# One of the four sums of each Strassen set is made in the PSUM bank, with an order chosen anew

## The chip, the core and the metric

The kernel runs on one core of one Trainium2 chip. A core has TensorE (PE in the profile, with its weight loads as PEld), VectorE (DVE), ScalarE (ACT), GpSimd (POOL) and SyncE (SP), which each run their own list of instructions in order and wait for one another through semaphores. TensorE writes its products into PSUM banks; VectorE and ScalarE read those banks and write SBUF, and may write a bank too. Transfers between HBM and SBUF are issued here by SP's queue. The metric is the device time of one execution in microseconds (us), the lower the better; a figure for a kernel is the median of its runs.

## The reference, cut to what matters

Attention over 4 batches, 8 heads, 768 positions and a head size of 64, in which a query sees 8 global keys and a local band of 96; then a gated layer without a nonlinear function on the 3072 tokens of 512 features that come out.

```python
scores = scale * np.matmul(q, k.transpose(0, 1, 3, 2)) + bias      # bias falls with distance
scores = np.where(is_global | is_local, scores, -1e9)
a = softmax(scores)                                                # over the keys
attn = np.matmul(a, v)
x = attn.transpose(0, 2, 1, 3).reshape(3072, 512)
out = ((x @ w_a) * (x @ w_b)) @ w_out                              # w_a, w_b 512x1536, w_out 1536x512
```

## The kernel before, in words

The 3072 tokens are cut into six blocks u of 512, and the weights into six pieces fp. A table of 18 passes takes a piece and some blocks at a time. Matmuls run on numbers that are cut into a high and a low part (`xf`, `w`, `hh`, `hl`), so that a float32 product is made of three matmuls: high by high, low by high, high by low. The cut is a CAST (`copy`, L660, to ScalarE at L663 or to VectorE at L665) and a subtraction on VectorE (`tt`, L670, whose instruction is at L673).

The first two passes multiply plainly (`project_plain`, matmul L1458). All later ones use `project` (L1532), which makes the two projections of a piece and a block by seven products in Strassen's manner instead of eight; one such set is named u_fp in the rows, as 5_4, and there are 30 of them. Each product is 12 matmuls of 128x256 (`product` L1430, matmul L1436) into one of two PSUM banks, `al` and `ga`. What comes out of a bank goes to SBUF tiles `s` (three for each set, numbered 0, 1 and 2 in the rows: s1, su and s5 in the code) by `take`, a copy that ScalarE or VectorE does, and by `add`, which adds the bank onto such a tile (VectorE, L1547). The gated product `h` is then made half by half on VectorE, from the two halves of an `s` tile (`times`, L673) or, for one half, from the bank and a copy `sa` of the bank's other half (L1588).

`h` is multiplied by the last weights in `back` (L1614, matmul L1628, tile `acc`), or in the late passes 10 to 17 in Strassen's manner too (`strong_back`, matmul L1688, tiles `m_acc`, `m_psS`, `m_psA`; `quad_back`, L1808, at the very end).

The attention is made in granules, a token block and a pair of heads each, named u_p, as 1_3: scores on TensorE (L1064, `ps`), mask and maximum on VectorE (L1032), exponent on ScalarE (L1048), division by the sum (L1168 on ScalarE in 128x168 pieces, or L1170 on VectorE in one 128x672), a transpose on VectorE (L1198, `tt`), a trip through memory by DMA (`mir`, read back as `px` and `py`), and the values on TensorE (L528, `pa`). Granules of the later blocks lie between the products of the earlier ones.

All these steps are put in one list by a table written in the program, `ORDER` (L127): its numbers say in which order the planned steps are emitted, and each engine works its own steps in that order. A second table, `ON_SCALAR` (L338), names the steps that may go to either ScalarE or VectorE and are to go to ScalarE. No step moves at run time: an engine whose next instruction has to wait stands still.

The core of a set in `project`:

```python
self.product(due, al, w["A11"], x["B11"], True)
take(due + 1 * st, s1, al)
self.product(due + 1 * st, ga, w["A12"], x["B21"], True)
add(due + 2 * st, s1, ga)
```

## Time and profile before

| what | value |
|---|---|
| median of 3 runs | 680.6 us (679.3 to 683.14) |
| the profiled execution: its own time | 684.21 us |
| its span, first to last instruction | 682.4 us |
| granted TensorE clock, mean | 0.994 of full speed |
| busy PE, PEld | 663.9 us (97%), 615.3 us (90%) |
| busy DVE | 631.9 us (93%) |
| busy ACT | 406.6 us (60%) |
| share of PE in the chain that ended last | 79% |

The profile is of one execution, which took 684.21 us by the same clock as the three runs; its span leaves out 1.8 us ahead of the first and behind the last instruction. A busy share is a mean over stages, so the stages are read apart. Records of neighbouring matmuls overlap: twelve matmuls of 128x256 show as 1.59 us although the next twelve begin 1.42 us after them.

### The profile page before, as it was taken

The numbers are of one execution on the slowest core, as the hardware profiler recorded it, in microseconds if no ns is written. First come the engines' busy times: TensorE is split into PE (matmuls) and PEld (weight loads), VectorE is DVE, ScalarE is ACT, GpSimd is POOL, SyncE is SP. The second block draws the span as 40 slices with busy tenths as digits, with TensorE's granted clock in tenths as the row PEclk, the third lists the DMA queues.
The fourth block names the chain that finished last, engine by engine and source line by source line (L and its number), as shares of the span: only waits on it lengthen the run. The fifth ranks groups of instructions, "written<-read, shape, count | busy, mean of one in ns | idle before, by whom it ended". The sixth has DMA issues, their size and how long they took to land.

```text
span 682.4 us, 17619 instructions
## 1 busy us (share of the span) xinstructions
PE 663.9 (97%) x6735; PEld 615.3 (90%) x6735; DVE 631.9 (93%) x1642; ACT 406.6 (60%) x1105; POOL 11.1 (2%) x32
## 2 busy tenths in 40 slices
PE   6899899999999999999999999999999999999996
PEld 5689797779898998999999998999999999999996
DVE  8999898899999999989988978899999999999976
ACT  8998784688894766637666467256455445442310
POOL 1000000000000000000000000000000000000000
PEclk9899998999999999999999999999999999999999
DMA  8879999989999899999998799754545652413252
GB/s 337 296 265 278 314 281 318 325 253 351 332 330 307 297 311 276 311 277 320 263 292 285 232 277 258 221 190 167 152 127 155 211 191 93 126 62 125 67 166 83
DMA packets 78991, 162.48 MB, mean 238 GB/s; under 512 B 7794, under 2 KB 36594, under 8 KB 74546
## 3 DMA queue, kind: packets, MB, share of 16 engines
q1 hardware_dynamic: 78610, 161.05, 74.1%
q8 instruction: 55, 0.90, 0.6%
q14 instruction: 38, 0.31, 0.1%
q10 hardware_dynamic: 288, 0.22, 0.1%
HBM read 108.81 MB, written 52.43 MB: 236 GB/s over the span
## 4 chain that ended last, share of the span: by engine, by line
PE 79%; DVE 6%; issue 5%; DMA 5%; ACT 2%; SPq 1%; POOL 0%; DVEq 0%; ACTq 0%; POOLq 0%
PE al L1436 24%; PE ga L1436 18%; PE acc L1628 14%; PE m_acc L1688 6%; PE m_psS L1688 3%; PE ps L1064 2%; DMA dw_O<-wm 2%; PE ps_al L528 2%; PE m_psA L1688 1%; ACT t L1048 1%; DMA py<-mir 1%; PE ps_ga L528 1%; DMA wr<-wts 1%; PE acc L1808 1%; DVE tt L1198 1%
## 5 line engine op out<-in xcount | busy, mean ns | idle before, releaser
L1628 PE MATMUL acc<-w_O,hh 128*128 128x512 f32 x320 | 114.0, 401 | 0.0
L1436 PE MATMUL al<-xf_T,w_S 128*128 128x256 f32 x720 | 95.7, 282 | 0.0
L1436 PEld LDWEIGHTS al<-xf_T,w_S 128*128 128x128 f32 x720 | 90.3, 188 | 1.3 <-ACT s L663 0.4
L1048 ACT ACTIVATE t<-t,sm 128x168 f32<-128x168 f32 x192 | 81.9, 430 | 13.9 <-DVE sm L1032 13.7
L1628 PEld LDWEIGHTS acc<-w_O,hh 128*128 128x128 f32 x320 | 60.2, 188 | 12.9 <-DVE w_O L673 0.3
L1628 PE MATMUL acc<-w_O,hl 128*128 128x512 f32 x160 | 63.0, 394 | 0.0
L663 ACT COPY s<-al 128x512 f32<-128x512 f32 x55 | 32.1, 584 | 36.7 <-PE al L1436 36.4
L1436 PE MATMUL ga<-xf_T,w_S 128*128 128x256 f32 x360 | 48.2, 283 | 0.2
L1032 DVE CUSTOM_DVE_ANT_0 t<-ps,mask 128x168 f32<-128x168 f32 x160 | 47.8, 326 | 0.6 <-PE ps L1064 0.4
L1436 PE MATMUL al<-xf_T,w_A 128*128 128x256 f32 x360 | 48.1, 283 | 0.1
L1436 PE MATMUL al<-xf_B,w_A 128*128 128x256 f32 x360 | 48.1, 283 | 0.0
L1436 PE MATMUL ga<-xf_B,w_S 128*128 128x256 f32 x360 | 47.9, 282 | 0.0
L1436 PE MATMUL ga<-xf_B,w_A 128*128 128x256 f32 x360 | 47.8, 282 | 0.0
L1436 PEld LDWEIGHTS al<-xf_B,w_A 128*128 128x128 f32 x360 | 45.7, 188 | 1.9 <-DVE sm L1032 0.6
L1168 ACT ACTIVATE t<-t,sm 128x168 f32<-128x168 f32 x124 | 43.2, 425 | 7.0 <-DVE sm L1148 6.8
L1436 PEld LDWEIGHTS al<-xf_T,w_A 128*128 128x128 f32 x360 | 45.5, 188 | 1.3 <-DVE xf_T L673 0.2
L1436 PEld LDWEIGHTS ga<-xf_T,w_S 128*128 128x128 f32 x360 | 45.1, 188 | 1.2 <-DVE s L1547 0.7
L1436 PEld LDWEIGHTS ga<-xf_B,w_S 128*128 128x128 f32 x360 | 45.2, 188 | 0.6
L1547 DVE TENSOR_TENSOR s<-ga,s 128x512 f32<-128x512 f32 x60 | 40.9, 682 | 4.9 <-PE ga L1436 4.8
L1436 PEld LDWEIGHTS ga<-xf_B,w_A 128*128 128x128 f32 x360 | 45.1, 188 | 0.3
L1198 DVE STREAM_TRANSPOSE tt<-t 128x512 f32<-128x512 f32 x80 | 40.3, 550 | 1.4 <-ACT t L1168 1.0
L1064 PEld LDWEIGHTS ps<-qk 64*64 64x64 f32 x960 | 29.4, 141 | 11.5 <-issue 6.2
(383 smaller groups left out, 1535.6 us busy)
## 6 DMA issues: line engine op xcount, KB each, us to landing
wr<-wts SPq DMA_DIRECT2D x21, 1024.0 KB, 7.5
mir<-tt SPq DMA_DIRECT2D x80, 192.0 KB, 4.0
vt<-vd SPq DMA_DIRECT2D x24, 512.0 KB, 6.8
qk<-qk SPq DMA_DIRECT2D x20, 576.0 KB, 7.1
X<-dx SPq DMA_DIRECT2D x11, 1024.0 KB, 6.1
part<-o SPq DMA_DIRECT2D x36, 256.0 KB, 3.7
wl_S<-dw_S SPq DMA_DIRECT2D x36, 256.0 KB, 4.1
px<-mir SPq DMA_DIRECT2D x20, 448.0 KB, 7.1
```

Of the source, the lines that this page charges most:

```text
L528: self.main.nc.tensor.matmul(self.banks[s][64 * h : 64 * h + 64, o : o + 64], self.vt[rows, v0 : v0 + 64], src[rows, 2 * s : 2 * s + 2, 2 ...
L663: self.nc.scalar.copy(out(), src())
L1032: lambda e: nc.vector.tensor_tensor_reduce(t[:, i, h], bank[:, c0 : c0 + KW], self.mask[pair][:, h, kind], -0.125, 3.0e38, ALU.add, ALU.mi ...
L1048: lambda e: nc.scalar.activation(t[:, i, h], t[:, i, h], AF.Exp, bias=sm[:, 0, j : j + 1], scale=-1.0, accum_out=sm[:, 1, j : j + 1],),
L1064: nc.tensor.matmul(bank[64 * s : 64 * s + 64, c0 + c : c0 + c + w], qk[rows, q0 + 64 * s : q0 + 64 * s + 64], qk[rows, k0 + k : k0 + k + w ...
L1168: nc.scalar.mul(flat()[:, j], flat()[:, j], sm[:, 3, j : j + 1])
L1198: nc.vector.transpose(dst[:, :, e0 : e0 + n], src[:, :, c0 : c0 + 32 * n].rearrange("p j (e k) -> p j e k", e=n),)
L1436: self.nc.tensor.matmul(bank[:, ab * HT : ab * HT + HT], w[:, a, (2 * ab + c) * P : (2 * ab + c) * P + P], x[:, b, c], start=first, stop=F ...
L1547: lambda e: nc.vector.tensor_tensor(s[:, :], bank[:, :], s[:, :], op=ALU.add),
L1628: self.nc.tensor.matmul(acc[i][:, :], a[:, rows], w[:, b], start=first and f == 0 and k == 0, stop=False, skip_group_check=True,)
L1688: self.nc.tensor.matmul(bank[:, c * HT : c * HT + HT], fa(k, c * P, c * P + P), fb(l), start=first, stop=False, skip_group_check=True,)
L1808: self.nc.tensor.matmul(acc[i][:, j * HT : j * HT + HT], a[:, rows], ws[j][0](b), start=f == 0 and j == 0 and k == 0, stop=False, skip_gro ...
```

## The change

Only `project` and the two tables are changed. In the code the order of the seven products is another: A11, S1, S2, S4, S3, A22, A12. The sum s1 = A11·B11 + A12·B21 is no longer made by a VectorE addition in SBUF. The first product is still taken out to `s1`, because `al` goes on to hold other sums; later `s1` is copied back into the bank `ga`, after su and s5 are done with it, and the product A12·B21 is added onto it there (`fresh` is False). The half of `h` that came from `s1` is now made from the bank, as the other one was: a copy `sg` of half a bank, and a multiplication of the other half by it (`across`). `sa` and `sg` share one buffer.

```diff
-        self.product(due, al, w["A11"], x["B11"], True)
-        take(due + 1 * st, s1, al)
-        self.product(due + 1 * st, ga, w["A12"], x["B21"], True)
-        add(due + 2 * st, s1, ga)
-        self.product(due + 2 * st, al, w["S2"], x["T2"], False)
-        take(due + 3 * st, su, al)
-        self.product(due + 3 * st, ga, w["S1"], x["T1"], True)
-        take(due + 4 * st, s5, ga)
-        self.product(due + 4 * st, al, w["S3"], x["T3"], False)
-        add(due + 5 * st, s5, al)
-        self.product(due + 5 * st, ga, w["S4"], x["B22"], False)
-        add(due + 6 * st, su, ga)
-        self.product(due + 6 * st, al, w["A22"], x["T4"], False)
-        sa = self.sbuf([P, HT], F32, "sa", "sa" + n, 1)
-        self.copy(due + 7 * st, lambda: sa[:, :], lambda: al[:, :HT], HT, [al], [sa], psum=True)
...
-        times(due + 3 * st, 0, 0, s1)
-        times(due + 6 * st, 1, 1, s5)
-        times(due + 7 * st, 0, 1, su)
-        op(
-            due + 7 * st,
-            lambda e: nc.vector.tensor_mul(h[1][:, :HT], al[:, HT:], sa[:, :]),
...
+        def across(due, f, bank, name):
+            s = self.sbuf([P, HT], F32, "sa", name + n, 1)
+            self.copy(due, lambda: s[:, :], lambda: bank[:, :HT], HT, [bank], [s], psum=True)
+            op(
+                due,
+                lambda e: nc.vector.tensor_mul(h[f][:, :HT], bank[:, HT:], s[:, :]),
+                [bank, s],
+                [(h[f], 0)],
+                dve=dve(HT),
+            )
+
+        self.product(due, al, w["A11"], x["B11"], True)
+        take(due + 1 * st, s1, al)
+        self.product(due + 1 * st, ga, w["S1"], x["T1"], True)
+        take(due + 2 * st, s5, ga)
+        self.product(due + 2 * st, al, w["S2"], x["T2"], False)
+        take(due + 3 * st, su, al)
+        self.product(due + 3 * st, ga, w["S4"], x["B22"], False)
+        add(due + 4 * st, su, ga)
+        self.product(due + 4 * st, al, w["S3"], x["T3"], False)
+        add(due + 5 * st, s5, al)
+        self.copy(due + 5 * st, lambda: ga[:, :], lambda: s1[:, :], T, [s1], [ga])
+        self.product(due + 5 * st, al, w["A22"], x["T4"], False)
+        across(due + 6 * st, 1, al, "sa")
+        self.product(due + 6 * st, ga, w["A12"], x["B21"], False)
+        across(due + 7 * st, 0, ga, "sg")
+        times(due + 5 * st, 0, 1, su)
+        times(due + 6 * st, 1, 1, s5)
```

`ORDER` and `ON_SCALAR` are other numbers throughout; both have no row that could be read by itself. What they do is seen in the lists of the engines. TensorE's lists have the same matmuls and weight loads in both. Lines of the changed kernel are 4 to 7 higher than those of before for the same code (L1436 is L1440, L1547 is L1551, L663 and L665 are L667 and L669).

The first place is set 5_4 on TensorE. A name such as `al5_4_3602` is the bank `al` of set 5_4; the operand behind the comma names the weight part (A11, S2, and so on). Before:

```order
994 L1436 MATMUL ga5_4_3588<-xf1_B21_290313_3476,w4_A12_163548_2638 128x256 x12
995 L1436 MATMUL al5_4_3602<-xf1_B11_290313_3518,w4_A11_163548_2226 128x256 x12
996 L1628 MATMUL acc3_0_3264<-w4_O1_163548_3110,hh4_4_1_3288 128x512
997 L1628 MATMUL acc3_0_3264<-w4_O1_163548_3110,hl4_4_1_3299 128x512
998 L1628 MATMUL acc3_0_3264<-w4_O1_163548_3110,hh4_4_1_3288 128x512
999 L1436 MATMUL al5_4_3602<-xf1_T2_290313_3511,w4_S2_163548_2862 128x256 x12
1000 L1436 MATMUL ga5_4_3588<-xf1_T1_290313_3540,w4_S1_163548_2859 128x256 x12
1001 L1436 MATMUL al5_4_3602<-xf1_T3_290313_3635,w4_S3_163548_2711 128x256 x12
1002 L1436 MATMUL ga5_4_3588<-xf1_B22_290313_3623,w4_S4_163548_3004 128x256 x12
1003 L1436 MATMUL al5_4_3602<-xf1_T4_290313_3688,w4_A22_163548_2504 128x256 x12
```

The same place on TensorE in the changed kernel:

```order
997 L1440 MATMUL al5_4_3593<-xf1_B11_290313_3455,w4_A11_163548_2225 128x256 x12
998 L1440 MATMUL ga5_4_3611<-xf1_T1_290313_3523,w4_S1_163548_2432 128x256 x12
999 L1440 MATMUL al5_4_3593<-xf1_T2_290313_3544,w4_S2_163548_2943 128x256 x12
1000 L1440 MATMUL ga5_4_3611<-xf1_B22_290313_3571,w4_S4_163548_2738 128x256 x12
1001 L1440 MATMUL al5_4_3593<-xf1_T3_290313_3663,w4_S3_163548_2843 128x256 x12
1002 L1440 MATMUL ga5_4_3611<-xf1_B21_290313_3631,w4_A12_163548_3090 128x256 x12
1003 L1440 MATMUL al5_4_3593<-xf1_T4_290313_3674,w4_A22_163548_2371 128x256 x12
```

The product A12 on `ga` has moved from the head of the set to a place behind S4, with one product, S3, between the two.

The second place is VectorE at that set. In the changed kernel (`s5_4_0` is s1, `s5_4_1` is su, `s5_4_2` is s5):

```order
662 L677 TENSOR_TENSOR xT4_1_290313_3666<-X_61,xT2_1_290313_3302 128x512
663 L1551 TENSOR_TENSOR s5_4_1_3669<-ga5_4_3611,s5_4_1_3669 128x512
664 L669 COPY ga5_4_3611<-s5_4_0_3624 128x512
665 L677 TENSOR_TENSOR xf1_T4_290313_3674<-xT4_1_290313_3666,xf1_T4_290313_3674 128x512
666 L1551 TENSOR_TENSOR s5_4_2_3634<-al5_4_3593,s5_4_2_3634 128x512
```

and in the kernel before:

```order
666 L1547 TENSOR_TENSOR s5_4_2_3686<-al5_4_3602,s5_4_2_3686 128x512
667 L673 TENSOR_TENSOR w3_O0_183130_3724<-wl3_O0_183130_3616,w3_O0_183130_3724 128x512
668 L673 TENSOR_TENSOR hl4_3_0_3733<-h4_3_0_3621,hh4_3_0_3706 128x512
669 L745 ISA wm3_5_3460<-wr3_4_3317,wm3_5_3460 128x1024
670 L1547 TENSOR_TENSOR s5_4_1_3670<-ga5_4_3588,s5_4_1_3670 128x512
```

The addition of S4's product onto su is now followed at once by the copy into `ga`, which here stands on VectorE; before, nothing of the set followed it on that bank.

The third place is SP's queue at granule 1_3, where `wr` is a load of raw weights, `qk` and `vt` are loads for later granules, and `part` is a store. Before:

```order
54 L653 DMA qk0_59<-qk 128x1152
55 L653 DMA mir1_3_1654<-tt1_3_1544 32x6x256 x4
56 L689 DMA wr5_2_1673<-wts 128x1024
57 L653 DMA qk1_60<-qk 128x1152
58 L653 DMA px0_272<-mir1_3_1654 112x1024
59 L653 DMA py0_134<-mir1_3_1654 64x512 x2
60 L653 DMA vt2_1_1772<-vd 128x1024
```

In the changed kernel:

```order
55 L657 DMA qk1_60<-qk 128x1152
56 L657 DMA mir1_3_1583<-tt1_3_1542 32x6x256 x4
57 L693 DMA wr5_2_1611<-wts 128x1024
58 L657 DMA vt2_1_1656<-vd 128x1024
59 L657 DMA px0_290<-mir1_3_1583 112x1024
60 L657 DMA py0_140<-mir1_3_1583 64x512 x2
```

The load of `qk1` has moved ahead of the four stores of `mir1_3`, and the load of `vt2_1` from behind the reads of `px` and `py` to a place ahead of them.

## Rows read from the trace of the kernel before

**Rows 1.** The page's busy time (share of the span) and instructions of each engine.

```profile
PE 663.9 (97%) x6735; PEld 615.3 (90%) x6735; DVE 631.9 (93%) x1642; ACT 406.6 (60%) x1105; POOL 11.1 (2%) x32
```

**Rows 2.** By stretch: length, busy PE, PEld, DVE, ACT, POOL, granted clock, DMA share, GB/s.

```profile
100.00:120.00 20.00, 18.36 (x184) 14.60 (x184) 16.78 (x34) 9.39 (x20) 0.00 (x0) 0.91 1.02 324
120.00:220.00 100.00, 100.00 (x1030) 86.80 (x1030) 96.58 (x255) 76.89 (x207) 1.58 (x5) 1.00 0.98 318
220.00:320.00 100.00, 99.90 (x1140) 90.98 (x1139) 93.67 (x242) 61.30 (x176) 2.01 (x5) 1.00 0.94 299
320.00:460.00 140.00, 139.92 (x1477) 129.71 (x1477) 125.05 (x326) 79.69 (x231) 2.40 (x6) 1.00 0.85 253
460.00:560.00 100.00, 99.95 (x839) 99.54 (x838) 97.70 (x224) 52.10 (x113) 0.00 (x0) 1.00 0.54 169
560.00:660.00 100.00, 99.97 (x835) 99.32 (x834) 95.46 (x225) 38.62 (x87) 0.00 (x0) 1.00 0.32 104
```

**Rows 3.** Waits of PE, whole span: who waited for whom: us in total, times, longest.

```profile
PE pa L528 <- DMA py<-mir: 1.6, 1, 1.6
PE ps L1064 <- DMA qk<-qf: 1.6, 1, 1.6
PE ga_1(1,)_1235 L1458 <- DVE h L1504: 1.1, 1, 1.1
```

**Rows 4.** The chain that ended last, 470 to 500 us: start us, us, what.

```profile
475.12 1.43 PE al L1436 x12
476.54 1.58 PE ga L1436 x12
```

**Rows 5.** VectorE by line and shape: count, busy us, mean ns, idle before and releaser.

```profile
L1547 DVE TENSOR_TENSOR s<-ga,s 128x512 f32<-128x512 f32 x60 | 40.9, 682 | 4.9 <-PE ga L1436 4.8
L673 DVE TENSOR_TENSOR h<-s 128x256 f32<-128x256 f32 x90 | 37.3, 418 | 0.7
L1588 DVE TENSOR_TENSOR h<-al,sa 128x256 f32<-128x256 f32 x30 | 12.6, 419 | 4.3 <-ACT sa L663 4.0
L1170 DVE TENSOR_TENSOR t<-t,sm 128x672 f32<-128x672 f32 x9 | 7.7, 856 | 0.5
L665 DVE CAST xf_T<-xT 128x512 fp32r<-128x512 f32 x10 | 4.1, 413 | 0.7 <-PE al L1436 0.7
L665 DVE COPY s<-al 128x512 f32<-128x512 f32 x5 | 3.4, 684 | 0.0
```

**Rows 6.** ScalarE by line and shape, columns as in rows 5.

```profile
L663 ACT COPY s<-ga 128x512 f32<-128x512 f32 x30 | 17.5, 584 | 12.3 <-PE ga L1436 10.8 <-DVE w_O L673 0.8 <-DVE h L673 0.7
L663 ACT CAST xf_T<-xT 128x512 fp32r<-128x512 f32 x38 | 23.5, 620 | 10.5 <-DVE xT L673 10.4
L663 ACT COPY sa<-al 128x256 f32<-128x256 f32 x26 | 9.7, 372 | 47.6 <-PE al L1436 47.5
L1168 ACT ACTIVATE t<-t,sm 128x168 f32<-128x168 f32 x124 | 43.2, 425 | 7.0 <-DVE sm L1148 6.8
```

**Rows 7.** Timeline of PE and VectorE, 499 to 508 us: start us, us, what.

```profile
499.76 1.35 PE L1436 MATMUL ga<-xf_B,w_S 128*128 128x256 f32 x10
504.52 1.59 PE L1436 MATMUL ga<-xf_B,w_A 128*128 128x256 f32 x12
...
502.65 0.68 DVE L1547 TENSOR_TENSOR s<-ga,s 128x512 f32<-128x512 f32 x1
506.26 0.68 DVE L1547 TENSOR_TENSOR s<-ga,s 128x512 f32<-128x512 f32 x1
506.86 0.42 DVE L673 TENSOR_TENSOR xo<-wl_O 128x256 f32<-128x256 f32 x1
```

**Rows 8.** The chain that ended last, 60 to 126 us: start us, us, what.

```profile
98.76 5.13 DMA mir<-tt
...
105.03 7.48 DMA py<-mir
...
114.59 4.45 PE al_0(0, 1)_1793 L1458 x12
...
119.74 3.04 PE al_1(0, 1)_1835 L1458 x12
```

More of the change, by code (lines that the diff above doesn't have):

```diff
@@ L1581, in times @@
             )
-        times(due + 3 * st, 0, 0, s1)
-        times(due + 6 * st, 1, 1, s5)
-        times(due + 7 * st, 0, 1, su)
-        op(
-            due + 7 * st,
-            lambda e: nc.vector.tensor_mul(h[1][:, :HT], al[:, HT:], sa[:, :]),
-            [al, sa],
-            [(h[1], 0)],
-            dve=dve(HT),
-        )
+        def across(due, f, bank, name):
[24 more added lines that the diff above has]
+        times(due + 5 * st, 0, 1, su)
+        times(due + 6 * st, 1, 1, s5)
         parts = []
```

490 rows, old and new, of tables (ON_SCALAR, ORDER) are left out of this document.

## The prediction

> **What bounds the kernel now.** I read the busy time of the engines first, then the same by stretch, then PE's list of waits, then the chain that ended last. The page puts PE at 663.9 us, 97% of the span, and VectorE at 631.9 us, 93% [rows 1]: two engines near full, and the change is about the second. Which of the two sets the end is read from the stretches: from 120 to 660 us PE is busy for 100.00 + 99.90 + 139.92 + 99.95 + 99.97 = 539.7 of 540 us, while VectorE lies between 89% and 98% [rows 2]. A busy record by itself doesn't prove that matmuls follow without loss, since neighbouring records overlap. So I look at their spacing: in the chain a product of 12 matmuls takes 1.43 us, and only now and then 1.58 [rows 4]. No wait of PE is listed from behind 115 us; the ones that are come from the head, 1.6 for the read-back of `py`, 1.6 for the first queries, 1.1 for a reader of a bank [rows 3]. The reader should see here that PE sets the time for four fifths of the span, that it has next to nothing to gain there, and that what can be won or lost lies ahead of 120 us or in waits that are not there yet.
>
> The Trainium skill, Perfetto Trace Analysis, section Identifying the Most-Contended Engine, says that matmul busy time is a poor measure of TensorE's headroom and that the busy share of the weight loads should be taken. By that the share is 90% in place of 97% [rows 1]. I come back to it as a rival.
>
> **The change part by part.** The matmuls are the same in number and shape, so PE's own work costs 0 more and 0 less. All other terms are what PE is made to wait or no longer waits.
>
> VectorE's work. I compared the lists of VectorE in the two orders, kind by kind. Gone: 30 additions `s<-ga,s` at 682 ns, -20.5 us. Exchanged: 30 multiplications `h<-s` at 418 for 30 from the bank at 419, 0 [rows 5]. New or moved over from ScalarE by the table: 4 copies into `ga`; 4 `sg` and 2 more `sa` copies at about 0.42, +2.5; 5 more 512-wide copies out of banks (3 of them `s<-ga`) at 684, +3.4; 12 more 512-wide casts at 413, +5.0; 4 more divisions of 128x672 at 856, +3.4; some small ones, -0.8 [rows 5]. The copy into a bank has no row in the trace of before. From the nearest rows it costs 413 ns (SBUF to SBUF, the CAST) to 684 ns (bank to SBUF, the COPY), for four 1.7 to 2.7 us; I take 684, because one side is a bank. Sum: -20.5 + 2.7 + 2.5 + 3.4 + 5.0 + 3.4 - 0.8 = -4.3 us. Four fifths of the relief is spent at once on work that comes over from ScalarE.
>
> The Trainium skill, VectorE: DVE Perf Modes, section Why PSUM operands drop a tier, says that an operand in PSUM holds a float32 operation at the plain rate. For these four copies that means the higher price, 2.7 us, and without the rule the sum would be -5.3 instead of -4.3.
>
> ScalarE's work. New: 26 copies into `ga`, between 584 (bank to SBUF) and 620 ns (SBUF to SBUF), +15.2 to +16.1 us, and 26 copies `sg` at 372, +9.7 [rows 6]. Gone to VectorE: 16 division pieces at 425, -6.8; 12 casts at 620, -7.4; 5 copies at 584, -2.9; 2 `sa`, -0.7; others about 0. Sum about +7.5. ScalarE is busy for only 60% of the span [rows 1], so the total costs nothing; where its work is dense is the head, below.
>
> What the bank has to hold. This is the new chain: S4's last matmul on `ga`, then the addition onto su (VectorE), then the copy of s1 into `ga`, and only then the first matmul of A12. What PE has between S4 and A12 is the cover. Counted from the new order, at 1.43 us for a product: one product in 2 sets (4_3 and 5_4, both with the copy on VectorE behind the addition), 2.09 to 2.14 us in 8 sets, 2.8 to 2.9 in 7, and 3.5 to 10 in the other 13. The need, in the best case: in the timeline an addition begins 0.15 us after the records of its product end (506.26 against 504.52 + 1.59) and the next instruction of VectorE 0.60 after it (506.86) [rows 7]; 0.15 + 0.60 + 0.68 + some 0.1 for the signal (my estimate, from that same 0.15) is 1.53 us. Since the records of a product reach 0.16 past the start of the next (1.59 against 1.43), one product covers 1.27. So 0.26 short, twice: +0.5 us. In a bad case the addition comes as late as the one at 502.65, 1.54 us after its product's last record (499.76 + 1.35): the need is 2.9, and against the cover less 0.16 the loss is 1.65 in the 2 sets, 0.95 in the next 8, 0.3 in the next 7, 13.0 us in all. Queued behind a copy that waits in ScalarE's list are the takes of the next product, and PE waits for those in turn. Ends +0.5 and +13.0; I take +0.5, because the lists put the additions of the two tight sets where VectorE has few rows ahead of them, and because additions and takes with one product as cover stand in before as well, without a wait of PE from 120 us on.
>
> What VectorE's relief gives back. From 120 to 660 us PE's records leave 0.3 us idle [rows 2]. Products that take 1.58 instead of 1.43 lose 0.15 each [rows 4]; were that so in 20 places, that would be 3 us. Ends 0 and -3; I take -1.
>
> The head. PE lost 1.6 us in front of the values of granule 1_3, and behind it the clock fell: the granted clock is 0.91 of full in the stretch 100 to 120 us, so for a part of it at the lower of its two levels (1.2 instead of 2.4 GHz), and twelve plain matmuls took 4.45 us where the next twelve took 3.04, so 1.4 more [rows 2, 3, 8]. What PE waited for there is a trip through memory, 5.13 us out and 7.48 us back [rows 8], at a DMA share of 1.02 [rows 2]. In SP's list the 1024 KB of raw weights still stand between the way out and the way back, now with the 512 KB of `vt2_1` in place of the 576 KB of `qk1`: 64 KB less at 324 GB/s is 0.2 us. The scores and the values of 1_3 keep their places among PE's work within a microsecond. Ahead of the last division of 1_3 ScalarE has three more casts of `hh` (3 x 0.62 = 1.9 us, rows of the same width in [rows 6]) and half a microsecond of small rows more. I take 0; the ends are -5.0 (1.6 + 1.4, the 1.1 of [rows 3] and its like) and +2.4.
>
> The tail: behind the last product both orders have the same work on PE; 0.
>
> Sum: 684.2 + 0.5 - 1.0 + 0 = 683.7 us for the profiled execution's own time. That execution stands 0.5% above the median of the runs, so as a ratio: 680.6 x 683.7 / 684.2 = 680.1 us. About 0.5%, 3.4 us, is what a measurement of this kernel can tell from no change.
>
> **The rivals.** First, slower: the bank chain. The addition and the copy stand in line on `ga`, and PE waits for A12. It decides from a mean of 0.11 us in each of 30 sets (3.4 us); with half of these 17 sets as in the bad case it is +6.5, and with 1.0 given back 686.1 us. For it speaks that VectorE stays at 96% or so and additions do come 1.5 us late; against it, that the two tightest covers miss by 0.26 only.
>
> Second, slower: the head. ScalarE's 2.4 us more lie on the way to the division of 1_3, the trip through memory starts later and PE waits longer at the lower clock: without any relief 680.6 + 2.4 + 1.4 = 684.4. Against it: ScalarE is idle for half of the stretch from 100 us [rows 2], if a little late for this.
>
> Third, faster: the head loses its waits. If the trip through memory lands 1.6 us earlier, the wait and the slow matmuls go, and with the reader's wait it is -4 to -5, some 676 us. It needs the transfers ahead to be shorter by more than the 0.2 us that I find.
>
> Fourth, faster: PE has headroom from 120 us on, which shows in its weight loads: 86.80 of 100, 90.98 of 100 and 129.71 of 140 us [rows 2]. Then VectorE's 4.3 us could all come back: 676.3. By the Trainium skill, Perfetto Trace Analysis, as named above, that would be so. Against it: from 460 us on the share is 99%, with VectorE as full, and ahead of that the matmuls are of mixed widths, so that a load per matmul leaves more of the time without one.
>
> Fifth, the change doesn't do what it says: VectorE's relief goes to moved work and nothing of it reaches PE: 680.6 + 0.5 = 681.1, no difference.
>
> **How the numbers follow.** My forecast 0.56, the fifth 0.06: together 0.62 within 0.5%. The third 0.14 and the fourth 0.06: faster 0.20. The first 0.12 and the second 0.06: slower 0.18. The range for 8 in 10 reaches into both sides: down to 676.0, at the edge of the third and fourth, and up to 685.5, which takes in the second and half of the first. The forecast's own range is 678 to 683.
>
> **What would show it.** In the changed profile VectorE's busy time should be near 628 us, ScalarE's near 414, PE's unchanged to 1 us; `s<-ga,s` should stand at x30. A copy into `ga` on ScalarE should take 0.58 to 0.62 us. In PE's waits a product on `ga` that waits for a copy may appear with 0.2 to 0.3 us, twice; a total above 3 us there would make the first rival right and me wrong. From 120 us to the last product PE's stretches should be as full as before. If 100 to 120 us shows a granted clock of 1.00 and no wait of `pa`, the third rival holds.

## The result, and the profile after

The changed kernel takes 684.44 us (median of 17 runs, 682.67 to 686.93) against 681.32 for the kernel before (17 runs, 678.26 to 684.25) on the same chip. The ratio is 1.0052 [1.0034, 1.0070], so the change costs 3.1 us by the medians and 3.5 by the ratio, between 2.3 and 4.8 by the interval. The forecast was no change (680.1 us, its own range 678 to 683). The profiled execution of the changed kernel took 685.95 us, 1.5 above its median; that of before stood 2.9 above its own [rows 1 to 8 are of that one], so the two profiles lie only 1.7 us apart and stretches have to be compared over several profiles. The clock is not what sets the kernels apart: the mean granted clock of the 17 executions of the changed kernel is 0.996, and so is that of the 120 executions of the kernel before that were taken along with the experiments. In e15, e16 and e18 below some executions were disturbed; their ratios leave these out, their medians and spreads do not.

The busy time on the page after, which answers to [rows 1]:

```profile
PE 664.3 (97%) x6735; PEld 615.1 (90%) x6735; DVE 628.7 (92%) x1640; ACT 415.1 (61%) x1125; POOL 11.8 (2%) x32
```

VectorE has 3.2 us less to do and ScalarE 8.5 more, PE 0.4 more. By stretch, with the columns of [rows 2] and four stretches of the head added:

```profile
0.00:20.00 20.00, 14.61 (x217) 12.29 (x217) 15.62 (x79) 16.48 (x53) 2.40 (x10) 1.00 0.86 316
20.00:40.00 20.00, 16.00 (x222) 12.63 (x213) 19.59 (x66) 19.64 (x68) 1.44 (x3) 1.00 0.83 302
40.00:60.00 20.00, 18.95 (x234) 17.30 (x233) 19.87 (x69) 19.58 (x61) 0.49 (x1) 1.00 0.89 299
60.00:80.00 20.00, 18.32 (x201) 16.16 (x200) 16.43 (x43) 14.88 (x44) 0.31 (x1) 0.91 0.95 311
100.00:120.00 20.00, 19.44 (x200) 15.77 (x200) 18.62 (x39) 7.57 (x16) 0.00 (x0) 1.00 0.98 319
120.00:220.00 100.00, 99.59 (x1028) 86.27 (x1027) 96.16 (x256) 78.15 (x211) 2.21 (x5) 1.00 0.97 315
220.00:320.00 100.00, 99.22 (x1133) 90.19 (x1133) 92.05 (x237) 63.85 (x179) 1.93 (x5) 1.00 0.92 298
460.00:560.00 100.00, 99.69 (x835) 99.25 (x834) 95.84 (x219) 55.47 (x122) 0.00 (x0) 1.00 0.55 171
560.00:660.00 100.00, 99.85 (x836) 99.30 (x835) 94.41 (x224) 44.35 (x102) 0.00 (x0) 1.00 0.34 109
```

Two things are to be seen. Behind 120 us PE is a little less full in every row shown than in [rows 2], by 0.41, 0.68, 0.26 and 0.12 us. (Not all of that is the change's: e12 below, which has the order of before there, is 0.80 us idle from 220 to 320.) And between 40 and 80 us, which the prediction never looked at, PE stands idle for 2.7 us, while VectorE and ScalarE are full from 20 to 60. The rows of before for these two stretches are

```profile
40.00:60.00 20.00, 19.84 (x240) 18.32 (x241) 19.63 (x65) 19.36 (x58) 0.58 (x1) 1.00 0.75 248
60.00:80.00 20.00, 18.09 (x211) 16.03 (x210) 17.32 (x53) 14.74 (x46) 0.58 (x1) 1.00 0.93 292
```

so that one profile is idle there for 2.1 us too. The other four profiles with this head (e1, e4, e5 and e12) are idle for 0.2 us at most.

PE's waits from 120 us to the end, where before had none:

```profile
PE al L1440 <- DVE s L1551: 0.4, 1, 0.4
PE al L1440 <- DVE sm L1036: 0.4, 1, 0.4
PE ga L1440 <- DVE ga L669: 0.4, 2, 0.2
PE al L1440 <- ACT ga L667: 0.3, 1, 0.3
PE ga L1440 <- ACT ga L667: 0.2, 1, 0.2
```

The third row is the predicted wait, as predicted. It is read best at set 4_3 in the timeline of PE and VectorE:

```profile
236.59 1.12 PE L1440 MATMUL ga<-xf_B,w_S 128*128 128x256 f32 x8
237.55 1.60 PE L1440 MATMUL al<-xf_T,w_A 128*128 128x256 f32 x12
239.35 1.45 PE L1440 MATMUL ga<-xf_B,w_A 128*128 128x256 f32 x10 [0.20 <-DVE ga L669]
...
237.89 0.68 DVE L1551 TENSOR_TENSOR s<-ga,s 128x512 f32<-128x512 f32 x1
238.60 0.69 DVE L669 COPY ga<-s 128x512 f32<-128x512 f32 x1
```

S4's records end at 237.71; the addition begins 0.18 later, the copy 0.71 after it and lasts 0.69, and 0.06 later A12 begins: 1.64 us of chain, where the prediction had put 1.53. Without it A12 would have begun at 237.55 + 1.43 = 238.98; it lost 0.37. The same working gives 0.32 at 5_4, 0.31 at 15_0, 0.26 at 9_2 and 0.13 to 0.06 at three more sets, 1.5 us in seven sets. In the five sets with more cover VectorE has other work first: at 15_0 the addition begins 0.86 us after S4's records end, and at 9_2 a division of 0.85 us stands between the addition and the copy. The first and the fourth row are not the copy's doing. The first is A22 of 6_3, which loses 0.58 because VectorE's addition onto s5 comes late, behind a step that waits 0.8 us for a load of `X`; the fourth is an A22 near 530 us. In e3 below, where no copy goes into the bank, both start just as late, and no A12 loses anything.

PE's waits between 40 and 82 us; the profile of before has none of these there, but the 1.1 us for a reader of a bank [rows 3], 0.8 us in front of a `pa` with no releaser seen, and 0.2 for a ScalarE copy:

```profile
PE acc L1635 <- DVE hl L677: 1.3, 1, 1.3
PE al_1(1,)_890 L1462 <- ACT s_0(1,)_877 L667: 0.9, 1, 0.9
PE pa L532 <- DMA py<-mir: 0.3, 1, 0.3
```

Because single profiles differ, I worked out from the starts of the matmuls how late PE runs: for each matmul the distance to the next one, less the median distance of such pairs over all the profiles of this study. A sum of 30 us is no waiting time, as plain pairs of other kinds are in it too; only differences between kernels count. In us, by stretch of the trace:

| profile | 0–20 | 20–40 | 40–60 | 60–80 | 80–100 | 100–120 | to 120 | behind 120 |
|---|---|---|---|---|---|---|---|---|
| before | 8.4 | 10.2 | 3.5 | 4.4 | 2.3 | 6.1 | 34.9 | 29.2 |
| five profiles with the head of before, mean | 8.5 | 9.8 | 3.3 | 2.7 | 3.4 | 3.5 | 31.3 | |
| after | 9.1 | 9.6 | 4.5 | 5.8 | 2.0 | 3.8 | 34.9 | 31.3 |
| six profiles with the changed head, mean | 9.3 | 9.1 | 4.5 | 5.5 | 2.3 | 3.1 | 33.8 | |
| e3, no copy into the bank | 9.7 | 8.7 | 4.5 | 7.4 | 2.4 | 3.4 | 36.2 | 29.8 |
| e4, before without an addition | 8.7 | 9.2 | 3.2 | 2.7 | 3.4 | 3.0 | 30.2 | 26.9 |
| e12, before with one swap | 8.6 | 10.2 | 3.4 | 2.1 | 3.4 | 2.5 | 30.1 | 30.2 |

(The five are before, e1, e4, e5 and e12, from 29.2 to 34.9 up to 120 us; the six are after, e2, e3, e6, e7 and e8, from 31.4 to 36.2.) The first of the two means is 2.5 us lower, though single profiles of the two groups overlap. In 40–60 no profile of the one group reaches the other: 3.2 to 3.5 against 4.4 to 4.6.

### The profile page after: what moved, and what is told of

The parts are those of the page before. It is cut to its first block, busy times and chain, and to the rows that moved or that the text cites. A ratio compares the mean times of both kernels' runs of the same rounds, so it can differ in the third digit from the quotient of the medians.

```text
span 684.2 us, 17624 instructions
## 1 busy us (share of the span) xinstructions
PE 664.3 (97%) x6735; PEld 615.1 (90%) x6735; DVE 628.7 (92%) x1640; ACT 415.1 (61%) x1125; POOL 11.8 (2%) x32
## 4 chain that ended last, share of the span: by engine, by line
PE 70%; DVE 14%; DMA 5%; issue 5%; ACT 4%; SPq 1%; POOL 0%; DVEq 0%; ACTq 0%
PE al L1440 18%; PE ga L1440 14%; PE acc L1635 13%; PE m_acc L1695 5%; PE ps L1068 3%; PE m_psS L1695 2%; DMA dw_O<-wm 2%; PE ps_al L532 1%; DMA py<-mir 1%; PE pa L532 1%; DMA X<-dx 1%; DVE s L1551 1%; DVE xf_T L677 1%; DVE h L677 1%; ACT t L1052 1%
## 5 line engine op out<-in xcount | busy, mean ns | idle before, releaser
L1440 PE MATMUL al<-xf_T,w_S 128*128 128x256 f32 x720 | 95.5, 282 | 0.0
L1052 ACT ACTIVATE t<-t,sm 128x168 f32<-128x168 f32 x192 | 81.9, 430 | 16.7 <-DVE sm L1036 16.4
L1440 PEld LDWEIGHTS al<-xf_T,w_S 128*128 128x128 f32 x720 | 90.5, 188 | 1.4 <-ACT s L667 0.4
L1440 PE MATMUL ga<-xf_B,w_A 128*128 128x256 f32 x360 | 48.5, 284 | 0.6 <-DVE ga L669 0.4
L1440 PE MATMUL al<-xf_T,w_A 128*128 128x256 f32 x360 | 48.1, 283 | 0.7 <-DVE s L1551 0.4
L1440 PE MATMUL al<-xf_B,w_A 128*128 128x256 f32 x360 | 48.2, 283 | 0.4 <-DVE sm L1036 0.4
L1440 PE MATMUL ga<-xf_T,w_S 128*128 128x256 f32 x360 | 48.0, 282 | 0.0
L1440 PEld LDWEIGHTS al<-xf_B,w_A 128*128 128x128 f32 x360 | 45.5, 188 | 2.6 <-DVE sm L1036 0.8
L1440 PE MATMUL ga<-xf_B,w_S 128*128 128x256 f32 x360 | 47.8, 282 | 0.0
L1440 PEld LDWEIGHTS ga<-xf_B,w_A 128*128 128x128 f32 x360 | 45.2, 188 | 2.9 <-DVE ga L669 1.3
L667 ACT COPY s<-al 128x512 f32<-128x512 f32 x55 | 32.1, 584 | 25.4 <-PE al L1440 25.0
L1440 PEld LDWEIGHTS al<-xf_T,w_A 128*128 128x128 f32 x360 | 45.3, 188 | 1.7 <-DVE s L1551 0.6
L1440 PEld LDWEIGHTS ga<-xf_T,w_S 128*128 128x128 f32 x360 | 45.2, 188 | 0.5 <-DVE xf_T L677 0.2
L1440 PEld LDWEIGHTS ga<-xf_B,w_S 128*128 128x128 f32 x360 | 44.9, 188 | 0.0
L1172 ACT ACTIVATE t<-t,sm 128x168 f32<-128x168 f32 x108 | 37.6, 424 | 4.0 <-DVE sm L1152 3.9
L1068 PE MATMUL ps<-qk 64*64 64x168 f32 (+2 forms) x960 | 34.0, 277 | 2.8 <-DMA qk<-qf 1.9
```

The costliest lines, as they stand in the source:

```text
L667: self.nc.scalar.copy(out(), src())
L1052: lambda e: nc.scalar.activation(t[:, i, h], t[:, i, h], AF.Exp, bias=sm[:, 0, j : j + 1], scale=-1.0, accum_out=sm[:, 1, j : j + 1],),
L1068: nc.tensor.matmul(bank[64 * s : 64 * s + 64, c0 + c : c0 + c + w], qk[rows, q0 + 64 * s : q0 + 64 * s + 64], qk[rows, k0 + k : k0 + k + w ...
L1172: nc.scalar.mul(flat()[:, j], flat()[:, j], sm[:, 3, j : j + 1])
L1440: self.nc.tensor.matmul(bank[:, ab * HT : ab * HT + HT], w[:, a, (2 * ab + c) * P : (2 * ab + c) * P + P], x[:, b, c], start=first, stop=F ...
```

## The experiments

**One head with the other's body.** e1 is the changed kernel in the order of before up to its first Strassen product, e2 the kernel before with the changed head. The edit in short (in the file the table is a list of numbers):

```diff
-ORDER = order_of_this_kernel
+ORDER = head_of_other + [o for o in order_of_this_kernel if o not in head_of_other]
```

> The changed kernel with the order of before up to the first Strassen product (some 120 us) and its own order behind it. Bank theory (PE waits in front of A12 for the addition and the copy into the bank, some 2 us from 120 us on, the rest of the loss in the head): the loss shrinks to about 2 us, a ratio to before near 1.003, and the waits in front of A12 stay in the trace. Head theory (the new order loses its 3 us ahead of 120 us): a ratio of 1.000. If the head plays no part: 1.005 as in the changed kernel.

> The mirror image: the kernel before with the changed kernel's order up to the first Strassen product. Bank theory: only the head's part, about +1 us, a ratio near 1.0015. Head theory: the whole +3 us, 1.005. If the head plays no part: 1.000.

Measured: e1 688.16 us, 1.0093 [1.0064, 1.0122]; e2 685.86, 1.0069 [1.0035, 1.0103]. Both are slower than both kernels, so neither tells what the head alone costs. PE's waits of e1 from 130 us, at the seam of the two orders:

```profile
PE al L1437 <- DVE sm L1033: 1.8, 1, 1.8
PE ga L1437 <- DVE sm L1033: 1.2, 1, 1.2
PE al L1437 <- ACT s L664: 1.1, 1, 1.1
```

Neither kernel has waits of that size there. Between 120 and 200 us e1 runs 12.2 us late by the working above and e2 9.8, the other whole kernels 6.4 to 7.8. The seam hides the answer.

**The chain in the bank.** e3 copies s1 onto itself, and A12 starts its bank afresh; the two instructions stay, the dependence goes. e7 makes the copy into the bank twice.

```diff
-        self.copy(due + 5 * st, lambda: ga[:, :], lambda: s1[:, :], T, [s1], [ga])
+        self.copy(due + 5 * st, lambda: s1[:, :], lambda: s1[:, :], T, [s1], [s1])
...
-        self.product(due + 6 * st, ga, w["A12"], x["B21"], False)
+        self.product(due + 6 * st, ga, w["A12"], x["B21"], True)
```

```diff
-        self.copy(due + 5 * st, lambda: ga[:, :], lambda: s1[:, :], T, [s1], [ga])
+        def into(e):
+            for _ in range(2):
+                (nc.scalar.copy if e == "act" else nc.vector.tensor_copy)(ga[:, :], s1[:, :])
+
+        op(due + 5 * st, into, [s1], [ga], act=act(T), dve=dve(T, True))
```

> The changed kernel, in which the copy of s1 is written onto s1 itself instead of into the bank ga, and A12 starts afresh (one half of h is then wrong). The work of the engines stays about the same, but A12 waits only for the addition of S4. Bank theory: the waits of PE for a copy into ga vanish and some 2 us come back, a ratio near 1.002. Head theory: 1.005 as before.

> The changed kernel with each copy of s1 into the bank made twice in a row on the same engine. Bank theory: about nine A12 products already wait, so each waits some 0.5 us longer, and others begin to: +4 to +6 us against the changed kernel, a ratio to before near 1.012, with the waits in front of A12 grown in the trace. If the copies lie beside PE's work: ScalarE's 15 us more cost nothing, 1.005.

Measured: e3 683.78 us, 1.0021 [0.9990, 1.0052]; e7 693.55, 1.0167 [1.0124, 1.0210]. In e3 no product waits for a copy into `ga`, and behind 120 us PE runs 1.5 us less late than in after (29.8 against 31.3); the ratios differ by 0.0031, 2.1 us, with intervals that overlap. (e10 below, with the same body as after, runs 30.6 us late behind 120 us, so profiles alone differ by 0.7.) The 1.5 us that seven products lose one by one in after, and in e3 none, are the best figure. In e7 the chain shows in PE's waits, behind 120 us:

```profile
PE ga L1440 <- ACT ga L1595: 4.8, 8, 1.2
PE ga L1440 <- DVE ga L1595: 2.7, 3, 0.9
PE al L1440 <- DVE h L1577: 0.4, 1, 0.4
```

Eleven products on `ga` wait 7.5 us, and the kernel loses 9.1 us to after by the medians, 7.8 by the ratios, more than was expected. So the copy is on the path, for some 1.5 us, and a second one of 0.6 us in each set costs about five times that: the covers of more sets no longer reach.

**What VectorE's relief is worth.** e4 leaves the 30 additions onto s1 out of the kernel before, 20.5 us of VectorE [rows 5, half of the x60]. e8 keeps the changed order but makes s1's sum on VectorE as before, without a copy into the bank.

```diff
-        add(due + 2 * st, s1, ga)
+        op(due + 2 * st, lambda e: None, [ga], [s1], dve=dve(T))
```

```diff
-        self.copy(due + 5 * st, lambda: ga[:, :], lambda: s1[:, :], T, [s1], [ga])
+        op(due + 5 * st, lambda e: None, [s1], [ga], act=act(T), dve=dve(T, True))
...
-        self.product(due + 6 * st, ga, w["A12"], x["B21"], False)
-        across(due + 7 * st, 0, ga, "sg")
+        self.product(due + 6 * st, ga, w["A12"], x["B21"], True)
+        op(
+            due + 7 * st,
+            lambda e: nc.vector.tensor_tensor(s1[:, :], ga[:, :], s1[:, :], op=ALU.add),
...
```

> The kernel before without the 30 additions onto s1 (one half of h lacks a product): VectorE has 20.5 us less to do, order and PE's work as before. If VectorE's relief is worth next to nothing because PE is full (my step on the relief, -1 us): a ratio of 0.998 to 1.000. If PE has headroom that VectorE's lateness eats (the fourth rival): several us, 0.99 or lower.

> The changed order with the arithmetic of before: A12 starts afresh on ga, VectorE adds it onto s1 in SBUF where the copy sg stood, no copy into the bank. VectorE has some 19 us more than in the changed kernel, in places that were not chosen for it. If VectorE's relief is worth 0.07 us for each us, as the run without additions says, then -1.6 for the chain and +1.3 for the work: about the changed kernel's time, 1.004 to 1.005. If the new order leans on the relief: 1.01 or more.

Measured: e4 680.45 us, 0.9982 [0.9957, 1.0007]; e8 695.66, 1.0210 [1.0163, 1.0257]. 20.5 us off VectorE bring 0.0018 x 681.3 = 1.2 us and at most 2.9, and by the interval perhaps nothing: 0.06 us for each, at most 0.14. The other way round it is dear: e8 is some 11 us slower than after, with waits of PE on VectorE's `s` (3.5 us, 4 times) and on a ScalarE take (2.0 us, twice). So the changed order, with the additions where e8 puts them, leans on the lighter VectorE, and the order of before hardly uses it.

**The heads by themselves.** e5 and e6 are the two kernels cut off behind the same 826 steps, which are those that both have in their heads (a few of them are moved up, so that these come first); all later steps are left out.

```diff
-            for o in order:
+            for o in order[:826]:
```

> Only the steps that both orders have ahead of the first Strassen product (826 of them: the first two passes and what goes with them), in the order of before; all later steps are left out, so there is no result. It is to be compared with the next run, which does the same steps in the changed order. If the head plays no part the two medians agree within 0.5 us.

> The same 826 steps in the changed kernel's order, all later steps left out. Bank theory with a part for the head: 1 to 2 us above the run before, since the copies were worth 1.6 of the 3.1 us. Head theory: 3 us above. Head without a part: equal.

Measured: e5 160.35 us (159.64 to 160.92), e6 164.60 (164.37 to 166.36): 4.2 us, with no overlap. In the profiles the last matmul ends at 153.9 and 157.7, and 3.7 and 5.1 us of each span lie behind it; that 1.4 is how the cut-off lists end and not a cost of the whole kernel, so 2.8 of the 4.2 remain. (The last matmuls of these two profiles lie 3.8 us apart; that e5 ran below its median there is a part of it.) None of the 826 steps is a Strassen product, so the sum in the bank has no part in this: what the head loses comes of the order chosen anew. By stretch, of e5 and then of e6:

```profile
0.00:20.00 20.00, 14.39 (x219) 12.28 (x219) 16.60 (x83) 16.90 (x53) 2.37 (x10) 1.00 0.91 333
20.00:40.00 20.00, 16.49 (x213) 13.05 (x214) 19.76 (x66) 19.71 (x66) 0.46 (x2) 1.00 0.85 301
40.00:60.00 20.00, 20.00 (x239) 18.45 (x239) 19.88 (x68) 19.33 (x61) 0.57 (x1) 1.00 0.85 267
60.00:80.00 20.00, 20.00 (x230) 18.16 (x229) 19.55 (x58) 16.41 (x53) 1.20 (x2) 1.00 0.98 324
```

```profile
0.00:20.00 20.00, 14.59 (x193) 12.11 (x193) 15.06 (x78) 15.97 (x50) 1.96 (x9) 1.00 0.83 307
20.00:40.00 20.00, 15.92 (x228) 12.66 (x226) 19.54 (x65) 19.60 (x69) 1.80 (x3) 1.00 0.81 298
40.00:60.00 20.00, 18.95 (x239) 17.11 (x236) 19.88 (x67) 19.51 (x59) 0.49 (x1) 1.00 0.87 297
60.00:80.00 20.00, 18.38 (x213) 16.30 (x213) 17.87 (x54) 15.95 (x49) 0.30 (x1) 1.00 0.95 309
```

The head alone shows what the whole kernel shows between 40 and 80 us: PE idle for 2.7 us, where with the order of before it is full in e5. PE's waits of e6 from 40 us on are the same two as in after:

```profile
PE acc L1632 <- DVE hl L674: 1.6, 1, 1.6
PE al_1(1,)_890 L1459 <- ACT s_0(1,)_877 L664: 0.9, 1, 0.9
```

**The waits in the head, one by one.** In after, the 1.3 us for `hl` come about so (timeline):

```profile
68.05 0.66 ACT L707 ACTIVATE wm<-wr 128x512 f32<-128x512 f32 x1 [2.01 <-DMA dw_O<-wm]
68.75 0.43 DVE L714 TENSOR_SCALAR wm<-wm 128x512 f32<-128x512 f32 x1 [1.63 <-ACT wm L707]
69.09 0.41 DVE L677 TENSOR_TENSOR hl<-h,hh 128x256 fp32r<-128x256 f32 x1
69.56 0.50 PE L1635 MATMUL acc<-w_O,hl 128*128 128x512 f32 x1 [1.30 <-DVE hl L677]
```

The half block `hl` is ready to be made, but in VectorE's list it stands behind a step on weights that waits for ScalarE, which waits for a store. e9 exchanges the two; e12 makes the opposite exchange in the kernel before.

```diff
-L714 TENSOR_SCALAR wm2_0_1083<-wm2_0_1083 128x512
 L677 TENSOR_TENSOR hl0_0_1_1046<-h0_0_1_858,hh0_0_1_931 128x256
+L714 TENSOR_SCALAR wm2_0_1083<-wm2_0_1083 128x512
```

```diff
-L673 TENSOR_TENSOR hl0_0_1_1076<-h0_0_1_886,hh0_0_1_1058 128x256
 L710 TENSOR_SCALAR wm2_1_1133<-wm2_1_1133 128x512
+L673 TENSOR_TENSOR hl0_0_1_1076<-h0_0_1_886,hh0_0_1_1058 128x256
```

> The changed kernel with one step moved in its order: on VectorE the subtraction hl0_0_1 (first half) stands ahead of the weight step wm2_0 instead of behind it. Step theory (PE's wait for hl near 68 us comes from VectorE standing at wm2_0, which waits for ScalarE, which waits for a store): the wait of 1.3 to 2.1 us goes, and the kernel gains about as much, a ratio to before near 1.003. Rival: the wait only moves, as VectorE is late there anyway: 1.005 with the same total of waits between 60 and 80 us.

> The mirror image in the kernel before: the subtraction hl0_0_1 (first half) behind the weight step wm2_1 on VectorE instead of ahead of it, nothing else. Step theory: PE waits for hl near 65 us and the kernel before loses 1 to 2 us, a ratio of 1.0015 to 1.003. Rival (the wait comes of the whole new head, not of this one place): 1.000.

Measured: e9 683.44 us, 1.0037 [1.0012, 1.0062]; e12 680.46, 1.0002 [0.9975, 1.0029]. In e9 the wait is gone, and in its place stands this one:

```profile
PE pa L529 <- DMA py<-mir: 2.5, 1, 2.5
```

PE comes to the values of granule 1_0 earlier, and the trip through memory is no sooner back. By the ratios e9 gains 1.0 us on after, within the intervals. In e12 nothing is lost, so this place alone is not the cause. e10 also moves the copy that the second wait is for, on ScalarE:

```diff
+L664 COPY s0_0_0(1,)_869<-al0_0_0(1,)_810 128x256
 L1169 ACTIVATE t1_0_757<-t1_0_757,sm1_0_758 128x168 x8
-L664 COPY s0_0_0(1,)_877<-al0_0_0(1,)_810 128x256
```

e11 is e10 with a block of `back` ahead of A12 in sets 6_4, 6_3, 9_2 and 15_1, as here on PE:

```diff
 L1437 MATMUL al9_2_6011<-xf2_T3_372251_5646,w2_S3_303517_5427 128x256 x12
...
+L1632 MATMUL acc7_3_5206<-w2_O1_303517_6027,hh8_2_1_5753 128x512
+L1632 MATMUL acc7_3_5206<-w2_O1_303517_6027,hl8_2_1_5836 128x512
+L1632 MATMUL acc7_3_5206<-w2_O1_303517_6027,hh8_2_1_5753 128x512
 L1437 MATMUL ga9_2_6032<-xf2_B21_372251_5661,w2_A12_303517_5435 128x256 x12
```

> As the run before, and on ScalarE the copy s0_0_0(1,) ahead of the eight division pieces of granule 1_0 instead of behind them. Step theory: the wait of 0.9 us near 53 us goes too, a ratio near 1.0015; what is left is the bank chain's 1.6 us. Rival: the division pieces come later by one copy, the memory trip of 1_0 too, and PE loses it there: no gain over the run before.

> As the run before, and in four sets (6_4, 6_3, 9_2, 15_1) one block of the back product moved ahead of A12, so that the addition and the copy have 0.7 us more cover. Bank theory: the waits in front of these four A12 (0.06 to 0.26 us each, with a slower start behind each, and the 0.58 us in front of A22 of 6_3) go, some 1 us: a ratio near 1.000. Rival: the blocks that were pulled ahead wait for their own operands: no gain.

Measured: e10 684.66 us, 1.0048 [1.0020, 1.0076]; e11 684.22, 1.0036 [1.0008, 1.0065]. Both head waits of after are gone in e10, and others stand there, from 40 us on:

```profile
PE pa L529 <- DMA py<-mir: 1.9, 1, 1.9
PE ps L1065 <- DVE sm L1033: 1.3, 1, 1.3
```

The stretch 40–60 is as late as before the move (4.6 against 4.5). e11 runs 30.4 us late behind 120 us against e10's 30.6: four more covers bring nothing that these runs can tell.

**What is ahead of the read-back.** On SP's queue the changed order has a load of `vt1_1` (512 KB) and a store of `dw1_A22` (256 KB) ahead of `px` and `py` of granule 1_0; before, the load came later and the store sooner. e13 is e10 with both behind the reads, e15 the kernel before with both in the changed kernel's places. e14 is e10 with the values of 1_0 one product later on PE.

```diff
-L654 DMA vt1_1<-vd 128x1024
 L654 DMA dw1_A21<-wm1_2 128x512
 L654 DMA mir1_0<-tt1_0 32x6x256 x4
-L654 DMA dw1_A22<-wm1_3 128x512
...
 L654 DMA py0<-mir1_0 64x512 x2
+L654 DMA vt1_1<-vd 128x1024
+L654 DMA dw1_A22<-wm1_3 128x512
```

```diff
-L529 MATMUL pa1_0_0<-py0,vt1_0 64x64 x2
...
 L1459 MATMUL al0_1_1(1,)<-xp0_0,w1_A21_0 128x256 x3
...
+L529 MATMUL pa1_0_0<-py0,vt1_0 64x64 x2
```

> The changed kernel with the two moves of e10, and on SP's queue the load vt1_1 (512 KB) and the store dw1_A22 (256 KB) behind the reads of px and py for granule 1_0 instead of ahead of them, as in the kernel before. Queue theory (PE stands in front of the values of 1_0 near 70 us, because py lands some 1.5 us later behind 768 KB more): the wait of about 2 us goes, and with it the slow stretch behind it; 60 to 80 us as full as before, a ratio near 1.002. Rival (PE comes to these values too early by its own order): the wait stays within 0.5 us.

> The changed kernel with the two moves of e10, and the values of granule 1_0 on PE one block of twelve plain matmuls (1.4 us) later. Both theories let the wait for py near 70 us go nearly; queue theory: the 1.4 us of cover take most of a wait of 1.9 us, a ratio near 1.003. If the wait comes back at the next memory trip or at scores: 1.005.

> The mirror image in the kernel before: vt1_1 ahead of the stores of mir1_0, and dw1_A22 between them and the reads of px and py. Queue theory: py lands about 1.5 us later and PE waits for it near 69 us, a ratio of 1.002 to 1.004. Rival: 1.000.

Measured: e13 684.16 us, 1.0045 [1.0023, 1.0067]; e14 684.29, 1.0049 [1.0020, 1.0078]; e15 683.75 (678.88 to 689.64), 1.0045 [1.0017, 1.0074]. So the two transfers do cost the kernel before some 3 us when they are put early (1.2 to 5.0 by the interval). PE's only wait of e15 from 40 to 160 us is this one:

```profile
PE pa L525 <- DMA py<-mir: 2.1, 2, 1.5
```

It doesn't say where the 3 us go. Of the 2.1 us, 1.5 stand at 1_3, where the other profiles with this head wait for `py` too (0.7 to 1.6 us); only 0.6 us, at 1_0, is new. Behind 160 us PE waits another 1.5 us for VectorE's `sm`, which the profile of before does not; whether that follows from the move was not shown. And taking the two transfers away from the changed kernel gives nothing back: in e13 the wait for `py` has gone, and PE waits for the scores instead.

```profile
PE ps L1065 <- DVE sm L1033: 1.3, 1, 1.3
PE ps L1065 <- ACT X L664: 0.9, 1, 0.9
PE pa L529 <- ACT wm L704: 0.8, 1, 0.8
```

**The same on the heads alone**, where 1 us can be told. e16 is e6 with the two transfers later, e17 is e6 with all four moves (e9, e10, e13 and e14), e18 is e5 with the two transfers early. Their edits are those above.

> The head alone in the changed order (826 steps, later ones left out, as e6 with 164.6 us), with vt1_1 and dw1_A22 behind the reads of px and py for granule 1_0. Queue theory: 1 to 2 us off, 162.6 to 163.6. Rival (VectorE and ScalarE are full ahead of 60 us, and PE waits at one place or another): within 0.5 us of 164.6.

> The same with all moves together: hl0_0_1 ahead of wm2_0, the copy s0_0_0(1,) ahead of the division pieces, the two transfers later, and the values of 1_0 one block later. If the four places are the head's loss: most of the 4.2 us that the truncated heads differ by comes back, 161 to 162. Rival: 163 or more, the waits move on.

> The head alone in the order of before (as e5 with 160.35 us), with vt1_1 and dw1_A22 ahead of the reads for 1_0, as in e15. Queue theory: 1 to 2 us more, 161.5 to 162.5. Rival: within 0.5 us of 160.35.

Measured: e16 164.63 us (163.3 to 166.15), e17 165.1 (164.39 to 165.93), against e6 with 164.60. By the ratios, 0.2410 [0.2397, 0.2424] and 0.2424 [0.2412, 0.2435] against 0.2420 [0.2406, 0.2434], e16 is 0.7 us better, within the intervals, and e17 no better. e18 has executions from 160.9 to 168.0, and its ratio to the kernel before, which rests on two of the six, is 0.2378 [0.2359, 0.2397], so 0.2378 x 681.3 = 162.0 us, against 0.2355 [0.2343, 0.2366] for e5: perhaps 1.6 us slower, with intervals that overlap. So the two transfers explain at most a small part of the difference of the heads.

## Why the prediction was wrong

**The counts and prices were right.** VectorE was to be busy for 628 us and is for 628.7, ScalarE for 414 and is for 415.1, PE's work is unchanged to 0.4. (VectorE's relief came out at 3.2 us, where the prediction added up 4.3.) The new instructions, with the columns of [rows 5]:

```profile
L667 ACT COPY ga<-s 128x512 f32<-128x512 f32 x26 | 15.3, 590 | 28.5 <-DVE s L1551 28.4
L667 ACT COPY sg<-ga 128x256 f32<-128x256 f32 x26 | 9.7, 372 | 18.0 <-PE ga L1440 13.2 <-DVE wm L732 1.5 <-DVE ft L677 1.1
L669 DVE COPY ga<-s 128x512 f32<-128x512 f32 x4 | 2.8, 690 | 0.1
L1551 DVE TENSOR_TENSOR s<-ga,s 128x512 f32<-128x512 f32 x30 | 20.5, 684 | 4.2 <-PE ga L1440 2.7 <-ACT s L667 0.9 <-ACT w_A L667 0.4
```

The copy into a bank, which no row of before showed, takes 590 ns on ScalarE (0.58 to 0.62 was said) and 690 on VectorE. There 684 was taken and the bounds were 413 and 684: it is a little dearer than the upper one. The rule of the Trainium skill, VectorE: DVE Perf Modes, section Why PSUM operands drop a tier, which pointed to the higher price, agrees.

**The head, taken at 0: this step failed.** The prediction asked only whether the trip through memory of granule 1_3, where before waited [rows 3, 8], would come sooner or later, and counted what ScalarE has ahead of one division. But a newly chosen order moves everything in the stretch, and PE's new loss lies at 40 to 80 us. Cut-off heads put it at 2.8 us or a little more, the mean lateness of six profiles against five at 2.5; of that, 40 to 80 us lose 4.0 and the stretch behind gives some back. Its size was inside the ends that were given (-5.0 to +2.4) or just past them; the value taken was wrong. The second rival had the head right, its mechanism not: in after PE waits for VectorE's `hl` and a ScalarE copy around granule 1_0, not longer at a lower clock for a trip of 1_3 that starts later. That its sum, 684.4 us, is the measured median is luck, and so is that the median lies within the range for 8 in 10 (676.0 to 685.5).

What the prediction named as the third rival's sign did appear: from 100 to 120 us the granted clock is 1.00, and PE doesn't wait for `py` there (0.6 us in front of `pa` have other releasers, or none that is seen). The clock is no doing of the change. e12, whose order is that of before but for one exchange, shows it too:

```profile
60.00:80.00 20.00, 20.00 (x228) 18.00 (x227) 19.57 (x62) 16.08 (x51) 1.21 (x2) 1.00 1.04 318
100.00:120.00 20.00, 19.31 (x138) 15.29 (x137) 18.29 (x35) 11.14 (x23) 0.00 (x0) 1.00 1.02 356
```

The lower clock of [rows 2], with the slow matmuls of [rows 8], belonged to the one execution that was profiled, which stood 2.9 us above the median of its kernel; in the other four with that head it is 1.00, and PE runs 2.5 to 3.5 us late from 100 to 120 us, against 6.1 in that one. The wait for `py` is the kernel's: it stands there in all five profiles with the head of before, with 0.7 to 1.6 us (0.7 in e12), and in none of the six with the changed head. So the third rival's wait did go, and PE had by then lost more than that at 40 to 80 us. The prediction read the whole stall of one execution as its kernel's and spent its look at the head on it.

**The chain in the bank, taken at +0.5: right mechanism, too small.** The two sets that were named lost 0.37 and 0.32 for 0.26 each, because the chain takes 1.64 and not 1.53 us. Five more sets, counted as covered by 2.1 us or more, lost 0.06 to 0.31, because VectorE came to the addition or the copy later than in the best case that was taken for all. The whole is 1.5 us in seven sets, none of which is left in e3: three times the term, but short of the 3.4 us from which the first rival was to decide, and its sign, more than 3 us of waits for a copy in front of A12, did not come (0.6 us).

**VectorE's relief, taken at -1.0: too much.** By e4's rate the 3.2 us that went from VectorE are worth 0.2 us, at most 0.5. The fourth rival, headroom by the weight loads (Trainium skill, Perfetto Trace Analysis, section Identifying the Most-Contended Engine), falls with it: by that rival, e4 should have gained much of its 20.5 us. A share of 90% in the mean did not mean that PE could take more; that mixed widths of the matmuls are the reason, as the prediction argued, was not tested.

Put together: 1.5 for the chain, less 0 to 0.5, plus 2.5 to 2.8 for the head is 3.5 to 4.3 us, against 2.3 to 4.8 measured. No version tried here beats the kernel before.

**What stays open** is which steps of the new head cost it its 2.5 to 2.8 us. Each wait that shows can be taken away, and PE then waits elsewhere: `hl`, then `py`, then the scores. All four moves together give nothing back that can be measured. That points to VectorE and ScalarE, which are 98 to 99% busy from 20 to 60 us in e5 and in e6, and to how much they have done by then; but it was not shown. VectorE's busy time in the first 20 us, 15.1 in e6 against 16.6 in e5, looked like the cause until e16, which has 16.5 there and is not measurably faster than e6.

## What to carry to other kernels

An order that is chosen anew has to be read through the whole stretch where two engines are full, not at the one place where the old profile shows a wait; and a slow stretch in one profile that stands above its kernel's median may not be the kernel's: look at a second profile before building on it. Relief of an engine beside a full one is worth what experiments like e4 say (here 1.2 us for 20.5), while a chain of drain, add and copy on a bank costs PE as soon as the products between don't cover it. Where whole kernels scatter by some us, kernels that are cut off behind the same steps can compare a stretch to about 1 us.

## What the runs showed of the hardware

A copy of 128x512 float32 from SBUF into a bank takes ScalarE 590 ns and VectorE 690. The same copy from SBUF to SBUF, which e3 makes in its place, takes them 618 and 420: with the bank as the target VectorE is 270 ns slower and ScalarE 28 ns faster. The clock was a matter of the execution: from 60 to 80 us it was granted at 0.91 in the profile of after and at 1.00 in that of e6, which runs the same steps there. So a part of that stretch ran in after at the lower of its two levels (1.2 instead of 2.4 GHz), although PE had been idle for the same 1.05 us in the stretch ahead of it in both.
